# The last third of w_a and w_b in 512-column rows and one four-tile step, unit 4's output a slot earlier, and the last store on ACT's queue

One core of a Trainium2 chip. The metric is the device time of one execution in microseconds (us). The profiler's span of the core (first to last instruction) is 1.7 to 1.9 us shorter than that time. The kernel before takes 233.46 us (median of the five runs beside the changed kernel, 233.22 to 233.78).

## The reference

A blockwise decaying linear attention over q, k, v of shape (4, 8, 768, 64) is followed by a bilinear feed-forward network (FFN) over its 3072 x 512 output:

```python
# per head, in blocks of 64; o: (3072, 512) once transposed and flattened
out[:, :, sl] = intra + inter          # masked (q k^T) v, plus q times the running state
kv_state = lam_block * kv_state + kb_dec^T vb
...
a = x @ w_a                            # (3072, 512) @ (512, 1536)
b = x @ w_b
return (a * b @ w_out).astype(np.float32)
```

All inputs are float32. The kernel computes in bfloat16 and accumulates in float32.

## The kernel before

Tokens go in 24 units of 128, in groups of 4, 1, 2, 4, 4, 4, 4, 1 units. For each group the FFN makes twelve a tiles and twelve b tiles of 128 hidden columns (f = 0..11), the products ab, and then the output. The attention of later units is woven in at numbered slots. Only group 0 meets the weights while they arrive: 12 chunks of w_a and w_b (512 KB each, 256 columns over the whole contraction), then six of w_out. Each is loaded as float32 and cast to bfloat16. Engines go by the profiler's names: PE is TensorE (matmuls), DVE VectorE, ACT ScalarE, POOL GpSimd; SP (SyncE) issues nearly all transfers.

```python
W_CHUNKS = (256,) * 6
W_STEPS = ((0, 1), (2,), (3,), (4,), (5,))
PLAN = {0: [..., (26, "T", 4), (29, "C", 5), (29, "S", 4), (30, "PV", 4), (34, "O", 4), ...], ...}

for cs in W_STEPS:                                   # order of the loads
    pending += [("a", c) for c in cs] + [("b", c) for c in cs]
...
def load_w(kind, c):                                 # (cut: w_out)
    t = wst_pool.tile([128, 1024], F32, name="wst", tag="wst")
    t = t[:, :KS * w].rearrange("p (k n) -> p k n", k=KS)
    nc.sync.dma_start(out=t, in_=r[:, :, w_off[c]:w_off[c + 1]])
...
# ffn, group 0                                       # (cut)
for i, cs in enumerate(W_STEPS):
    nxt = W_STEPS[i + 1][0] if i + 1 < len(W_STEPS) else None
    a_sbs = [a_part(f, ...) for f in fs]             # matmuls; ACT evacuates a
    if i == 0: cast_w("b", cs[1], "act")
    elif nxt:  cast_w("a", nxt, "dve")
    for n_f, (f, a_sb) in enumerate(zip(fs, a_sbs)):
        b_part(f, xT, gt, a_sb, ab)                  # matmuls; DVE multiplies
        hook(f)
    if nxt: cast_w("b", nxt, "act")
for c in range(FC // 2):                             # output, slots 12 to 35
    for t in range(n):
        out_mms(ops[t], ab, t, range(2 * c, 2 * c + 2))
        if c == FC // 2 - 1: store(u0 + t, ops[t], 0, d_model)   # ACT copy, kept
        hook(slot); slot += 1
```

Before the loop over groups, POOL casts the first chunk of w_a ("a0") in two halves, and DVE casts a1 and b0. The "O" hook makes a unit's attention output on TensorE and copies it to the x tile (xT) on ACT.

## Time and profile before

| | before |
|---|---|
| time, us | 233.46 (233.22 to 233.78) |
| span, us | 231.5 |
| TensorE (PE) busy | 225.1 us, 97% |
| DVE / ACT / POOL busy | 50% / 39% / 22% |
| clock granted to PE | 0.998 |

A line of the timeline is: start, duration, engine, line of the kernel, operation, output<-inputs, shapes, count, and in brackets how long the engine had rested and on what. A matmul's end is a model: with 512 columns the matmuls start 0.216 us apart but each is shown 0.38 us long. I therefore read PE by its starts. The prediction shows the page's shares, the stretches and group 0. One piece that it does not show becomes important below, the start of group 0: the cast of a0 on POOL, the cast of b0 on DVE, and the first a and b matmuls.

```profile
16.82 0.61 POOL L162 CAST wa_sb<-wst 128x512 bf16<-128x512 f32 x1 [0.53 <-DMA wst<-in_moe_w_a_dram]
17.92 3.62 PE L439 MATMUL a_ps<-xT,wa_sb 128*128 128x384 bf16 x20 [0.23 <-ACT xT L362]
20.60 0.69 DVE L165 CAST wb_sb<-wst 128x1024 bf16<-128x1024 f32 x1 [1.61 <-DMA wst<-in_moe_w_b_dram]
21.39 1.03 PE L439 MATMUL b_ps<-xT,wb_sb 128*128 128x512 bf16 x4
```

POOL and DVE both rest until their chunk has landed. The first half of a0 is cast by 17.43, 0.49 us ahead of PE's start at 17.92. The cast of b0 ends at 21.29, only 0.10 us before PE uses it. In this execution neither is late, but b0 runs close.

### The profile page before, as it was taken

How to read it: one execution, taken by the hardware profiler on the slowest of the kernel's cores; microseconds unless marked ns; L12 is line 12 of the kernel's file. 1: busy time of each engine (PE TensorE's matmuls, PEld its weight loads, DVE VectorE, ACT ScalarE, POOL GpSimd, SP SyncE). 2: the span in 40 equal slices, each digit the busy share in tenths (PEclk: the TensorE clock that was granted, in tenths of full speed). 3: DMA queues.
4: the chain of work that ended last, by engine and by line, in shares of the span. 5: the costliest groups of instructions: out<-in, count | busy, mean ns of one | idle time of the engine just before them, and what ended most of it. 6: DMA issues, size and time to landing. Idle time of an engine off the chain costs nothing.

```text
span 231.5 us, 4532 instructions
## 1 busy us (share of the span) xinstructions
PE 225.1 (97%) x1779; PEld 124.8 (54%) x1779; DVE 115.9 (50%) x204; ACT 90.9 (39%) x172; POOL 50.8 (22%) x65
## 2 busy tenths in 40 slices
PE   7799999999999999999999999999999999999994
PEld 2484444459688654554544454544554544444493
DVE  0894757536469726676334584334483313331050
ACT  3677563066473243342233333233333234332261
POOL 6071000336564333334301533001200000000000
PEclk9999999999999999999999999999999999999999
DMA  4999999998999999999869995239300220000311
GB/s 154 303 281 349 349 364 301 299 189 189 204 229 161 225 195 217 213 184 213 304 201 203 218 175 113 93 103 194 66 3 0 91 93 0 1 0 23 115 45 50
DMA packets 96422, 38.84 MB, mean 168 GB/s; under 512 B 83344, under 2 KB 91920, under 8 KB 96400
## 3 DMA queue, kind: packets, MB, share of 16 engines
q1 hardware_dynamic: 96256, 38.54, 72.5%
q8 instruction: 14, 0.23, 0.4%
q14 instruction: 8, 0.07, 0.1%
q10 hardware_dynamic: 144, 0.00, 0.0%
HBM read 28.32 MB, written 6.29 MB: 149 GB/s over the span
## 4 chain that ended last, share of the span: by engine, by line
PE 87%; DMA 4%; SPq 3%; ACT 2%; DVE 1%; issue 0%
PE a_ps L439 27%; PE b_ps L439 26%; PE op L472 23%; PE o_ps L355 3%; DMA q<-in_q_dram 3%; PE kq L313 2%; SPq L129 2%; PE o_ps L345 2%; DMA qf<-in_q_dram 2%; PE kvd L369 2%; ACT scratch L565 1%; PE tps L299 1%; SPq L145 1%; DVE scratch L542 1%; PE kq L590 1%; ACT xT L362 0%
## 5 line engine op out<-in xcount | busy, mean ns | idle before, releaser
L452 DVE TENSOR_TENSOR ab<-a_sb,b_ps 128x512 bf16<-128x512 bf16 (+2 forms) x96 | 52.3, 552 | 78.4 <-PE b_ps L439 57.4
L439 PE MATMUL a_ps<-xT,wa_sb 128*128 128x512 bf16 (+3 forms) x388 | 77.0, 324 | 0.4 <-ACT xT L362 0.4
L439 PE MATMUL b_ps<-xT,wb_sb 128*128 128x512 bf16 (+2 forms) x384 | 77.1, 326 | 0.0
L447 ACT CAST a_sb<-a_ps 128x512 bf16<-128x512 f32 (+2 forms) x96 | 45.6, 481 | 62.6 <-PE a_ps L439 61.3
L472 PE MATMUL op<-wo_sb,ab 128*128 128x512 bf16 (+2 forms) x312 | 65.6, 363 | 0.0
L439 PEld LDWEIGHTS <-wb_sb 128*128 128x128 bf16 x384 | 34.5, 98 | 28.6 <-DVE wb_sb L165 0.3
L439 PEld LDWEIGHTS <-wa_sb 128*128 128x128 bf16 x388 | 34.0, 98 | 28.7 <-issue 0.8
L472 PEld LDWEIGHTS <-ab 128*128 128x128 bf16 x312 | 28.7, 98 | 29.9
L330 DVE TENSOR_TENSOR m<-kq,lotri 128x512 bf16<-128x512 f32 x47 | 29.3, 682 | 17.8 <-PE kq L313 17.2
L262 POOL TENSOR_TENSOR qk<-kf,lp_k 128x512 bf16<-128x512 f32 x18 | 19.3, 1074 | 74.8 <-DMA kf<-in_k_dram 58.2
L267 POOL TENSOR_TENSOR qk<-qf,lp_q 128x512 bf16<-128x512 f32 x20 | 21.9, 1095 | 23.3 <-DMA qf<-in_q_dram 23.3
L467 ACT COPY o_sb<-op 128x512 f32<-128x512 f32 (+2 forms) x19 | 10.3, 541 | 34.0 <-PE op L472 34.0
L362 ACT CAST xT<-o_ps 128x512 bf16<-128x512 f32 x22 | 12.0, 590 | 18.0 <-PE o_ps L355 17.5
L401 DVE TENSOR_TENSOR st<-kvd,bdiag 128x512 bf16<-128x512 f32 x18 | 12.3, 682 | 4.2 <-PE kvd L369 3.6
L276 DVE CAST vb<-vf 128x512 bf16<-128x512 f32 x17 | 9.7, 570 | 0.0
L301 ACT COPY qkT<-tps 128x1024 bf16<-128x1024 bf16 x5 | 5.1, 1012 | 9.9 <-PE tps L299 9.9
L198 PE MATMUL idle<-idle_sb 128*128 128x128 bf16 (+1 forms) x31 | 6.8, 359 | 1.3 <-DVE idle_sb L193 1.3
L355 PE MATMUL o_ps<-m,vb 128*64 128x128 bf16 x192 | 7.8, 222 | 0.0
L276 POOL CAST vb<-vf 128x512 bf16<-128x512 f32 x7 | 4.4, 631 | 13.1 <-DMA vf<-in_v_dram 13.1
L345 PEld LDWEIGHTS <-st 128*128 128x128 bf16 x80 | 5.4, 98 | 2.8
L313 PE MATMUL kq<-qkT 64*128 64x128 bf16 x160 | 6.6, 218 | 0.0
L355 PEld LDWEIGHTS <-vb 128*64 128x64 bf16 x192 | 5.7, 109 | 1.4
(57 smaller groups left out, 86.5 us busy)
## 6 DMA issues: line engine op xcount, KB each, us to landing
vf<-in_v_dram SPq DMA_DIRECT2D x24, 256.0 KB, 4.9
qf<-in_q_dram SPq DMA_DIRECT2D x20, 256.0 KB, 4.6
kf<-in_k_dram SPq DMA_DIRECT2D x20, 256.0 KB, 4.7
out_dram<-o_sb SPq DMA_DIRECT2D x16, 256.0 KB, 2.0
wst<-in_moe_w_a_dram SPq DMA_DIRECT2D x6, 512.0 KB, 8.6
wst<-in_moe_w_b_dram SPq DMA_DIRECT2D x6, 512.0 KB, 8.7
wst<-in_moe_w_out_dram SPq DMA_DIRECT2D x6, 512.0 KB, 8.6
out_dram<-o_kept SPq DMA_DIRECT2D x7, 256.0 KB, 2.5
```

The lines of the kernel that those rows point to most:

```text
L262: eng_of(eng).tensor_mul(qk[:, 1], raw.pop((u, "k")), lp_k[:, u % NB].to_broadcast([128, H, D]))
L267: eng_of(eng).tensor_mul(U[u]["qk"][:, 0], raw.pop((u, "q")), lp_q[:, u % NB].to_broadcast([128, H, D]))
L276: eng_of(eng).tensor_copy(vb, vf)
L313: nc.tensor.matmul(kq[i][:, hp, :], lhsT=d["kT"][p, hp, :], rhs=d["qT"][p, hp, :], start=True, stop=True, skip_group_check=True)
L330: nc.vector.tensor_mul(m, kq[i], lotri_bc)
L355: nc.tensor.matmul(d["o"][p, hp, :], lhsT=d["vb"][:, 2 * hp + i, :], rhs=d["m"](i, hp), start=(first and hp == 0), stop=True, skip_group_c ...
L362: nc.scalar.copy(xT[:, :, col:col + BLK], o_ps)
L401: nc.vector.tensor_mul(st[:].rearrange("p hp i d -> p hp (i d)"), ps[:].rearrange("p hp i d -> p hp (i d)"), bdiag_bc)
L439: nc.tensor.matmul(ps[:, lo:hi], lhsT=w_sb[:, s, f * 128:(f + 1) * 128], rhs=xT[:, s, lo:hi], start=(s == 0), stop=(s == KS - 1), skip_gro ...
L447: nc.scalar.copy(a_sb[:, :gt], ps[:, :gt])
L452: nc.vector.tensor_mul(ab[:, f, :gt], a_sb[:, :gt], ps[:, :gt])
L472: nc.tensor.matmul(op[:, lo:hi], lhsT=ab[:, f, t * 128:(t + 1) * 128], rhs=wo_sb[:, f, lo:hi], start=(f == 0), stop=(f == FC - 1))
```

## The change

Its intent: load the last third of w_a and w_b with longer contiguous rows, let ACT make unit 4's x tile before its two last closing copies of group 0, and spare the hop to SP's queue. Chunks 4 and 5 cover 512 columns (2 KB rows) over one half of the contraction each, so the last four f tiles become one step; "O" of unit 4 moves from slot 34 to 33; the last of the three closing stores is issued by ACT.

```diff
-W_STEPS = ((0, 1), (2,), (3,), (4,), (5,))
+W_STEPS = ((0, 1), (2,), (3,), (4, 5))
+W_HALVES = (4, 5)
@@ PLAN[0]
-        (26, "C", 4), (26, "T", 4), (29, "C", 5), (29, "S", 4), (30, "PV", 4), (34, "O", 4),
+        (26, "C", 4), (26, "T", 4), (29, "C", 5), (29, "S", 4), (30, "PV", 4), (33, "O", 4),
@@
+    def w_part(w, c):
+        if c in W_HALVES:
+            j = W_HALVES.index(c)
+            return w[:, 2 * j:2 * j + 2, w_off[W_HALVES[0]]:]
+        return w[:, :, w_off[c]:w_off[c + 1]]
@@ load_w
-            nc.sync.dma_start(out=t, in_=r[:, :, w_off[c]:w_off[c + 1]])
+            if c in W_HALVES:
+                t = t.rearrange("p k n -> p (k n)").rearrange("p (k n) -> p k n", k=2)
+            nc.sync.dma_start(out=t, in_=w_part(r, c))
@@ cast_w
-            dst = (wa_sb if kind == "a" else wb_sb)[:, :, w_off[c]:w_off[c + 1]]
+            dst = w_part(wa_sb if kind == "a" else wb_sb, c)
@@ store
-        nc.sync.dma_start(out=out_r[row][:, lo:hi], in_=o_sb[:, lo:hi])
+        (queue or nc.sync).dma_start(out=out_r[row][:, lo:hi], in_=o_sb[:, lo:hi])
@@ ffn, group 0 (cut)
-                nxt = W_STEPS[i + 1][0] if i + 1 < len(W_STEPS) else None
+                nxt = W_STEPS[i + 1] if i + 1 < len(W_STEPS) else ()
-                elif nxt:
-                    cast_w("a", nxt, "dve")
+                else:
+                    for c in nxt:
+                        cast_w("a", c, "dve")
-                if nxt:
-                    cast_w("b", nxt, "act")
+                for c in nxt:
+                    cast_w("b", c, "act")
@@ ffn, last group
-                    store(u0 + t, op, lo, hi)
+                    store(u0 + t, op, lo, hi, nc.scalar if hi == d_model else None)
```

More of the change, by code (lines that the diff above doesn't have):

```diff
@@ L458, in store_kept, with store @@
         nc.sync.dma_start(out=out_r[row], in_=o_sb)
-    def store(row, op, lo, hi):
+    def store(row, op, lo, hi, queue=None):
         if row < g_u0[KEEP_GROUPS]:
@@ L491, in ffn @@
                     if i == 0 and n_f == 1:
-                        cast_w("a", nxt, "dve")
-                if nxt:
-                    cast_w("b", nxt, "act")
+                        cast_w("a", nxt[0], "dve")
+                for c in nxt:
+                    cast_w("b", c, "act")
             ops = [ps_bank("op", [128, d_model], F32, hold=True) for _ in range(n)]
```

## The prediction

> **What bounds the kernel now.** I read the page first, its busy shares and its row of slices, to see which engine could be the bound and where it rests.
>
> ```profile
> PE 225.1 (97%) x1779; PEld 124.8 (54%) x1779; DVE 115.9 (50%) x204; ACT 90.9 (39%) x172; POOL 50.8 (22%) x65
> PE   7799999999999999999999999999999999999994
> PEclk9999999999999999999999999999999999999999
> DMA  4999999998999999999869995239300220000311
> ```
>
> TensorE works for 225.1 of 231.5 us at full clock. It is short of work only in the first two slices and the last. The DMA engines are saturated over the first fifth of the span, where the weights arrive, so the change works on a resource that is full. Whether it is on the path is another question, answered by the table of stretches, which I cut at the boundaries of the first FFN group (22.64 is the first b matmuls after its start, 50.40 its last output matmuls).
>
> ```profile
> 22.64:50.40 27.76, 27.76 (x150) 12.83 (x148) 17.84 (x27) 11.51 (x17) 3.77 (x4) 1.00 1.09 310
> 50.40:51.30 0.90, 0.73 (x10) 0.28 (x5) 0.00 (x0) 0.90 (x3) 0.00 (x0) 1.00 0.99 225
> 51.30:225.50 174.20, 174.20 (x1386) 97.49 (x1386) 84.51 (x154) 63.64 (x127) 38.63 (x37) 1.00 0.66 136
> 228.20:231.50 3.30, 0.00 (x0) 0.00 (x0) 0.00 (x0) 0.25 (x1) 0.00 (x0) 0.83 0.24 72
> ```
>
> The first numbers are length and PE busy: no hole from 22.64 to 50.40, all of the stage that waits for weights; one of 0.17 us at 51; none afterwards; and 3.3 us of tail without a matmul. Because matmul ends are modelled, I checked the pace of starts as well, in the timeline of PE:
>
> ```profile
> 28.62 1.89 PE L439 MATMUL a_ps<-xT,wa_sb 128*128 128x512 bf16 x8
> 30.35 1.89 PE L439 MATMUL b_ps<-xT,wb_sb 128*128 128x512 bf16 x8
> 32.08 1.89 PE L439 MATMUL a_ps<-xT,wa_sb 128*128 128x512 bf16 x8
> 33.80 1.89 PE L439 MATMUL b_ps<-xT,wb_sb 128*128 128x512 bf16 x8
> 35.53 1.89 PE L439 MATMUL a_ps<-xT,wa_sb 128*128 128x512 bf16 x8
> 37.26 1.89 PE L439 MATMUL b_ps<-xT,wb_sb 128*128 128x512 bf16 x8
> 50.46 0.61 PE L472 MATMUL op<-wo_sb,ab 128*128 128x512 bf16 x2
> 51.23 0.38 PE L439 MATMUL a_ps<-xT,wa_sb 128*128 128x128 bf16 x4 [0.17 <-ACT xT L362]
> ```
>
> Eight 512-column matmuls start every 1.725 us, so 0.216 us each, throughout the weights' arrival: no weight is ever late. The only wait near the change is the last line: the next group's first matmul waits for the x tile of unit 4.
>
> **What the Trainium skill says.** "TensorE: Matmul & The Clock Gate", section "Wait — 56ns, not 53.3ns?", gives a warm start-to-start of 215.7 ns at 512 columns; the trace's 0.216 us agrees, so the stage cannot run faster. "Trainium Kernel Development and Optimization", Key Constraints, says that DMAs from several engines' queues share the same 16 DMA engines and that this saves only issue time. No transfer of the kernel before shows it for a store (ACT's queue carried only a 4 KB load). "Perfetto Trace Analysis", the HWDGE part of the per-instruction lifecycle, says that a DMA's issue leaves out the data's movement and that the closing semaphore write can take surprisingly long for HBM; here the last store's issue took 0.33 us but its landing 1.7 us. No page that I read gives a gain for 2 KB rows over 1 KB ones, so that is taken from this trace.
>
> **Part 1: rows of 512 columns.** Four of the twelve a and b loads keep their 512 KB but go from 1 KB rows (256 columns of 4 bytes) to 2 KB rows. The trace holds both sorts, in the DMA view of 22 to 31 us (a and b) and of 32.5 to 37 us (almost only w_out, which has 2 KB rows):
>
> ```profile
> DMA packets 3143, 3.14 MB, mean 349 GB/s; under 512 B 95, under 2 KB 3142, under 8 KB 3142
> DMA packets 921, 1.73 MB, mean 386 GB/s; under 512 B 51, under 2 KB 97, under 8 KB 921
> ```
>
> 4 x 0.524 MB takes 6.01 us at 349 and 5.43 us at 386 GB/s. What follows lands about 0.6 us earlier. Nothing on PE waited for it, so on the path this is worth 0.
>
> **Part 2: one step of four f tiles instead of two steps of two.** Same matmuls, same casts of 128x1024 (0.69 us on DVE, 1.05 on ACT; the w_out casts already have the new two-by-512 form at 0.69). The order of loads becomes a4 a5 b4 b5. Each a pair is now two halves of the contraction, so the very first f tile of the step needs both. The deadlines, with landing as issue plus the DMA view's time to landing: a4 20.97 + 8.6 = 29.57, and the next three before at 31.0, 32.6 and 34.05. In the new order and at 1.36 us each: a5 about 30.8, b4 32.2, b5 33.6 (estimates). PE starts the step at 32.08 and needs the second half of wa two matmuls later, 32.5; DVE casts a5 from 30.8 to 31.5, so there is 1.0 us to spare. ACT now casts b4 and b5 before it evacuates the step's four a tiles: b5 from 33.6 to 34.65, against a need at 35.53 + 0.43 = 35.96, 1.3 us to spare. The four a evacuations, 0.52 us apart, then run from 34.65 to about 36.8. Their banks come round again seven allocations later, the first of them for the last b tile at about 38.1, so they are free. The a pool has five buffers for four tiles. DVE gets its four products bunched behind that: the first about 36.7 instead of 34.9, the last about 39.9, and the w_out casts between them stay ahead of use by about 1 us (third one done about 41.2, needed at 42.4). Every delay is inside slack, so this is worth 0 too.
>
> **Part 3: unit 4's output one slot earlier** (34 to 33). Now ACT's queue at the end of the group is:
>
> ```profile
> 49.13 1.56 ACT L463 COPY o_kept<-op 128x512 f32<-128x512 f32 x3 [2.01 <-PE op L472]
> 50.57 0.62 ACT L362 CAST xT<-o_ps 128x512 bf16<-128x512 f32 x1
> 51.15 0.59 ACT L463 COPY o_kept<-op 128x512 f32<-128x512 f32 x1
> ```
>
> Three kept copies stand before the x tile and only one pair of output matmuls (0.43 us) follows it on PE. After, two copies stand before and two pairs follow. The last output pair's stream ends at 50.46 + 0.43 = 50.89, while the next group starts at 51.23, so the true hole is **0.34 us** (the 0.17 in brackets counts from the modelled end). New: the o_ps matmuls end 0.43 earlier, about 50.03; ACT is done with the second copy about 50.17; x runs 50.17 to 50.79; PE is ready at 50.89. The hole closes. The masks it reads are done at 49.02 and the o_ps matmuls that read them would start about 49.7, so no new wait. ACT's last two copies move behind x and the next group's first a evacuation starts at about 51.7 as before, though PE is 0.34 ahead; its banks are then reused with 0.3 us or so to spare. Gain 0.34 us, at risk by about 0.1.
>
> **Part 4: the last store from ACT's queue.** ACT's last copy starts at 228.18, takes 0.27 and ends at 228.45; SP issues at 228.48. The hop is 0.03 us, and SP is not late: its issues at 227.24, 227.81 and 228.48 each take 0.33. Landing and closing handshake remain. Gain 0.0 to 0.05, and ACT's one earlier issue took 0.41 us, so it may as well lose 0.08. I take 0.
>
> **Sum.** 0 + 0 - 0.34 + 0: 233.46 - 0.34 = 233.1 us, or 0.15% less.
>
> **Rivals.** (a) The a halves come late: if 2 KB rows on these strided tensors ran no faster than 1 KB ones, a5 would land at 31.0 and be cast by 31.7, still 0.8 us early. Only a landing over 1 us later would make PE wait; then about 234. Against: the first eight loads and their issue times stay the same, and w_out shows the rate. (b) The bunched ACT and DVE work holds PSUM banks and the output matmuls wait: 0.3 to 1 us lost, 233.4 to 234.1. For it: ACT's four evacuations finish only when PE is at the second b tile, and group 1's bank reuse is tight. Against: all slacks above are positive. (c) The early weights let q, k and v arrive earlier and later stages speed up. Against: from 51.3 to 225.5 PE has no hole, so it is worth 0. (d) The queue that has been idle since the start is slower or faster to finish than SP's: 0.3 us either way, 232.8 to 233.4. Nothing in the trace speaks for it but that nothing rules it out.
>
> **Range and chances.** Runs before spread from 233.22 to 233.78, about 0.3 to either side. With rivals (b) and (d) on either side of 233.1, I give 232.5 to 233.7. A change of 2% is 4.7 us: faster would take more than the whole 3.3 us tail together with the hole, and slower would take a PE wait longer than any slack here. 0.01 each, 0.98 within 2%.
>
> **What would show it.** Right: DMA near 386 GB/s through 29 to 37 us, no PE wait on wa_sb or wb_sb in the four-tile step, the start of group 1 at about 50.9 with no wait on xT, everything after it 0.3 us earlier, and the tail from the last matmul to the end 3.3 us as now. Wrong: a wait of PE or its weight loads on a5's cast, an output matmul waiting on a_sb or ab, a new hole in the first microseconds of group 1, or a tail that differs by over 0.2 us. If the time differs from 233.1 by more than 0.6 us, one of these slacks was misjudged.

## The result

The changed kernel took 233.41 us (233.08 to 233.85, 5 runs) beside 233.46 of before. The ratio is 0.9997, 95% interval 0.9981 to 1.0013: no difference that these runs resolve. A ratio here is the mean time of one kernel's fast runs over that of the other's in the same rounds, so it is not quite the ratio of the quoted medians.

The four loads, as forecast, run faster. The DMA view of 29 to 36 us of the changed kernel:

```profile
DMA packets 1403, 2.71 MB, mean 387 GB/s; under 512 B 81, under 2 KB 81, under 8 KB 1403
```

The hole at 51 us has gone. ACT's queue and PE's timeline there, to be held against the lines of the prediction:

```profile
49.49 1.07 ACT L472 COPY o_kept<-op 128x512 f32<-128x512 f32 x2 [2.01 <-PE op L481]
50.50 0.58 ACT L371 CAST xT<-o_ps 128x512 bf16<-128x512 f32 x1
51.03 1.07 ACT L472 COPY o_kept<-op 128x512 f32<-128x512 f32 x2
...
50.39 1.04 PE L481 MATMUL op<-wo_sb,ab 128*128 128x512 bf16 x4
51.26 0.39 PE L448 MATMUL a_ps<-xT,wa_sb 128*128 128x128 bf16 x4
```

Four output matmuls start at 50.39 and stream until 50.39 + 4 x 0.216 = 51.25, and group 1 follows at 51.26. Yet group 1 starts at 51.26 and not at the 50.9 that was forecast, hardly different from 51.23 before. The 0.36 us had been lost ahead of it, at the start of group 0 (POOL's cast of a0 and PE's first a matmuls):

```profile
17.60 0.61 POOL L171 CAST wa_sb<-wst 128x512 bf16<-128x512 f32 x1 [1.13 <-DMA wst<-in_moe_w_a_dram]
18.27 3.64 PE L448 MATMUL a_ps<-xT,wa_sb 128*128 128x384 bf16 x20 [0.39 <-POOL wa_sb L171]
```

Here a0 landed 0.78 us later than in the trace of before, POOL's first half ended at 18.21, and PE began at 18.27 instead of 17.92. The question for the experiments is whether the change did that, or chance. Apart from this wait on POOL's cast, the view of PE's waits lists none from 17.9 to 52 us in the changed kernel.

### The profile page after: what moved, and what is told of

Its sections match the earlier page's. It is cut to its first block, busy times and chain, and to the rows that moved or that the text cites. A ratio compares the mean times of both kernels' runs of the same rounds, so it can differ in the third digit from the quotient of the medians.

```text
span 231.6 us, 4530 instructions
## 1 busy us (share of the span) xinstructions
PE 225.1 (97%) x1779; PEld 124.8 (54%) x1779; DVE 114.1 (49%) x204; ACT 90.6 (39%) x172; POOL 50.1 (22%) x65
## 4 chain that ended last, share of the span: by engine, by line
PE 91%; SPq 4%; DMA 3%; issue 0%; POOL 0%; ACT 0%
PE a_ps L448 27%; PE op L481 27%; PE b_ps L448 27%; SPq L130 3%; DMA wst<-in_moe_w_a_dram 3%; PE o_ps L364 3%; PE kq L322 2%; PE o_ps L354 2%; SPq L220 1%; PE kvd L378 1%; PE tps L308 1%; PE kvd L399 0%; POOL wa_sb L171 0%; ACT o_sb L476 0%
## 5 line engine op out<-in xcount | busy, mean ns | idle before, releaser
L448 PEld LDWEIGHTS <-wb_sb 128*128 128x128 bf16 x384 | 34.5, 98 | 28.6 <-ACT wb_sb L169 0.2
L276 POOL TENSOR_TENSOR qk<-qf,lp_q 128x512 bf16<-128x512 f32 x20 | 21.0, 1051 | 22.3 <-DMA qf<-in_q_dram 22.3
L371 ACT CAST xT<-o_ps 128x512 bf16<-128x512 f32 x22 | 12.0, 588 | 18.0 <-PE o_ps L364 17.5
L285 DVE CAST vb<-vf 128x512 bf16<-128x512 f32 x17 | 8.2, 482 | 0.0
```

What stands on the lines that cost most here:

```text
L276: eng_of(eng).tensor_mul(U[u]["qk"][:, 0], raw.pop((u, "q")), lp_q[:, u % NB].to_broadcast([128, H, D]))
L285: eng_of(eng).tensor_copy(vb, vf)
L371: nc.scalar.copy(xT[:, :, col:col + BLK], o_ps)
L448: nc.tensor.matmul(ps[:, lo:hi], lhsT=w_sb[:, s, f * 128:(f + 1) * 128], rhs=xT[:, s, lo:hi], start=(s == 0), stop=(s == KS - 1), skip_gro ...
```

## The experiments

The span is cut at four points that every PE timeline shows: the first b matmul of group 0, the first a matmul of group 1, the end of the last output matmul (its line's start plus its duration), and the end of the span (the trace has it to 0.01 us). "First b" stands for the start because it contains every wait for a0, a1 and b0. The four numbers of a row add up to the span.

| kernel | slot | loads | last store | first b | first b to group 1 | group 1 to last matmul | tail | span | median time |
|---|---|---|---|---|---|---|---|---|---|
| before | 34 | old | SP | 21.39 | 29.84 | 176.91 | 3.39 | 231.53 | 233.46 |
| changed | 33 | new | ACT | 21.75 | 29.51 | 176.90 | 3.48 | 231.64 | 233.41 |
| slot_only | 33 | old | SP | 21.59 | 29.53 | 177.03 | 3.38 | 231.53 | 233.33 |
| loads_only | 34 | new | SP | 21.59 | 29.85 | 177.04 | 3.36 | 231.84 | 233.46 |
| store_only | 34 | old | ACT | 23.75 | 29.85 | 176.90 | 3.48 | 233.98 | 233.81 |
| store_again | 34 | old | ACT | 21.60 | 29.86 | 176.91 | 3.46 | 231.83 | 233.54 |
| after_again | 33 | new | ACT | 21.61 | 29.52 | 176.91 | 3.45 | 231.49 | 233.20 |
| slot_loads | 33 | new | SP | 21.97 | 29.51 | 176.91 | 3.36 | 231.75 | 233.28 |
| rows_1kb | 33 | four-tile step, 1 KB rows | ACT | 21.73 | 29.51 | 177.00 | 3.48 | 231.72 | 233.40 |
| late_half | 33 | new, a5 one load later | ACT | 21.51 | 30.03 | 176.91 | 3.45 | 231.90 | 233.56 |
| later_half | 33 | new, a5 two loads later | ACT | 21.54 | 31.14 | 177.34 | 3.46 | 233.48 | 235.33 |
| split_first | 33 | new, a0 and b0 in halves | SP | 22.39 | 29.52 | 176.91 | 3.38 | 232.20 | 233.60 |

Each row's first five numbers are from one execution, its median from that kernel's four to six. The first four experiments ran together on one chip, where before was 233.53 us (11 runs, 233.40 to 233.64).

**slot_only**: before, with `(33, "O", 4)`.

> The kernel before with unit 4's output at slot 33 and nothing else. Main theory: this is the only part of the change on the path. From the first a matmul of group 0 to the end of the last output matmul the trace shows 210.2 us before and 209.9 after; here 209.9, with no wait on xT at about 51 us, so the mean time is 0.3 us under before, as far as the start of group 0 (17.9 or 18.3 us, set by when the first w_a chunk lands) does not hide it. Rival (the loads or the four-tile step are what closed the hole): 210.2 with the 0.2 us wait on xT still there.

Measured: 233.33 us, ratio 0.9992 (0.9980 to 1.0004). The total by itself does not resolve the gain, since the interval includes 1. The stretch to group 1 does: it is 29.53 against 29.84 of before, and group 1 now starts right after the four output matmuls (50.24 + 4 x 0.216 = 51.10), so the slot alone closes the hole:

```profile
50.24 1.04 PE L472 MATMUL op<-wo_sb,ab 128*128 128x512 bf16 x4
51.12 0.39 PE L439 MATMUL a_ps<-xT,wa_sb 128*128 128x128 bf16 x4
```

The whole run from first a matmul to last output was 210.21, though, and not 209.9: this execution gave the gain back at b0. The cast of b0 on DVE and the first b matmuls of slot_only:

```profile
20.84 0.69 DVE L165 CAST wb_sb<-wst 128x1024 bf16<-128x1024 f32 x1 [1.50 <-DMA wst<-in_moe_w_b_dram]
21.59 1.04 PE L439 MATMUL b_ps<-xT,wb_sb 128*128 128x512 bf16 x4
```

The first a matmul was at 17.94, so PE was free at about 21.41 (the 3.47 us of before's first part); b0 landed 0.24 us later than in the trace of before, its cast ended at 21.53 and PE waited until 21.59. A further 0.12 us went after group 1, a spread that loads_only shares.

**loads_only**: the changed kernel with slot 34 and the last store on SP.

> The kernel before with the 512-column loads and the four-tile step, unit 4's output at slot 34, last store by SP. Main theory: the DMA rate rises to about 385 GB/s from 29 us on, but from the first a matmul to the last output matmul it is 210.2 us as before, with the xT wait still at 51 us; time equal to before within 0.1 us. Rival (bunched casts or the later products cost something that the slot gave back): over 210.4 us.

Measured: 233.46 us, ratio 0.9998 (0.9985 to 1.0011), 387 GB/s over 29 to 36 us, 29.85 us to group 1, and the wait on xT still there:

```profile
50.66 0.61 PE L481 MATMUL op<-wo_sb,ab 128*128 128x512 bf16 x2
51.44 0.38 PE L448 MATMUL a_ps<-xT,wa_sb 128*128 128x128 bf16 x4 [0.17 <-ACT xT L371]
```

In group 0 the loads and the four-tile step cost nothing and bring nothing. From the first a matmul to the last output matmul it is 210.36 us, between the 210.2 of the main theory and the 210.4 of the rival. The excess lies after group 1: the third number, 177.04, is on the upper side of a spread (176.90 to 177.04) that I did not explain. It is not put down to the loads, since slot_only has it without them and after_again and slot_loads do not have it with them.

**after_again**: the changed kernel unaltered.

> The changed kernel once more. Main theory: first a matmul to last output matmul 209.9 us again; the start of group 0 may be anywhere from 17.9 to 18.4 us since the instructions ahead of it are those of before and only the landing of the first w_a chunk moves it; time 0.0 to 0.35 us under before. Rival (the change itself makes that chunk land late): the start is at 18.3 in this run too, while slot_only and store_only start at 17.9.

Measured: 233.20 us (233.17 to 233.27), ratio 0.9988 (0.9976 to 0.9999). The first a matmul started at 17.91, so the late a0 of the first trace was not the change's doing; b0 was the late one here (cast from 20.86, first b at 21.61), and from the first a matmul to the last output matmul it is 210.13 us instead of the 209.9 expected. The same program thus gave a first b of 21.75 and of 21.61. Over the ten traces whose first loads came punctually (all but store_only and split_first), first b moves from 21.39 to 21.97 with the same instructions ahead of it, so this is chance in the landing of the first chunks. Before's trace, with 21.39, is the earliest of all.

**store_only and store_again**: before, with only the last store on ACT.

```diff
-                    store(u0 + t, op, lo, hi)
+                    store(u0 + t, op, lo, hi, nc.scalar if hi == d_model else None)
```

> The kernel before with the last store issued by ACT. Main theory: first a matmul to last output matmul stays 210.2 us; the tail from the last matmul's end to the end of the span stays 3.3 to 3.4 us (3.36 before, 3.44 after), time equal to before within 0.1 us. Rival (the hop to SP matters, or ACT's queue is slow to finish): tail shorter or longer by over 0.2 us.

Measured: 233.81 us (233.59 to 235.69), ratio 1.0027 (1.0004 to 1.0050), so the time was not within 0.1 us of before. The profiled execution was the one of 235.69 us; there the very first load of q landed late, and so everything did (PE's waits of store_only):

```profile
PE tq L554 <- DVE scratch L542: 2.5, 2, 2.2
```

Its tail, 3.48 (3.3 to 3.4 was expected), says more than its time. The other executions of this batch were slow too, and they left no trace.

> The kernel before with the last store issued by ACT, once more, since its first run started late and its five timed runs were 0.3 us over before. Main theory: the tail from the last matmul's end to the span's end is 3.45 to 3.5 us against 3.36 to 3.39 with SP (three profiles), so the time is 0.1 us over before; the rest of the first result was chance in the start. Rival (ACT's queue costs more than the profile shows): 0.25 us or more over before again.

Measured: 233.54 us beside 233.57, ratio 1.0001 (0.9989 to 1.0014). The excess did not come back. Why the first batch was slow stays open beyond its one trace. The tail does repeat: 3.36 to 3.39 us in the five profiles with SP, 3.45 to 3.48 in the seven with ACT, so ACT's store costs 0.09 us. The last copy and store, before and changed:

```profile
228.18 0.27 ACT L467 COPY o_sb<-op 128x128 f32<-128x128 f32 x1 [0.40 <-PE op L472]
228.48 0.33 SPq L468 DMA_DIRECT2D out_dram<-o_sb  x1
```

```profile
228.21 0.27 ACT L476 COPY o_sb<-op 128x128 f32<-128x128 f32 x1 [0.41 <-PE op L481]
228.50 0.36 ACTq L477 DMA_DIRECT2D out_dram<-o_sb  x1
```

From the copy's start to the issue it is 0.30 us with SP and 0.29 with ACT: there was no hop to save. The issue is 0.03 us longer, but that is already part of the time to the landing. From the start of the issue to the landing, the packed traces have 1.60 to 1.66 us in the five with SP and 1.65 to 1.68 in the seven with ACT (the views round both to 1.6 or 1.7), 0.03 us more on average. The other 0.05 us or so falls between the landing and the end of the span (1.41 us on average with SP, 1.46 with ACT). Why is not shown.

**rows_1kb**: the four-tile step with 256-column chunks over the whole contraction.

```diff
-W_HALVES = (4, 5)
+W_HALVES = ()
```

> The changed kernel with the same four-tile step and order of loads, but rows of 256 columns (1 KB) for all chunks, each over the whole contraction. Main theory: the DMA runs on at 349 GB/s until 32 us instead of rising to about 385 at 29, the w_out chunks land about 0.5 us later, and the time is that of the changed kernel within 0.1 us: row length is off the path. Rival (the faster rows are worth something): slower by 0.3 us or more.

Measured: 233.40 us beside 233.57; ratio of the means 1.0002 (0.9987 to 1.0018), since one of its four runs took 234.09. First b to group 1 is 29.51, as with 2 KB rows. The DMA moved 368 GB/s over 29 to 36 us (1 KB rows first, then w_out) against 387. Over 29 to 32.5 us, where nearly all rows are 1 KB in rows_1kb and 2 KB in the changed kernel, with the same step and order, the views show (rows_1kb, then changed):

```profile
DMA packets 1184, 1.23 MB, mean 350 GB/s; under 512 B 45, under 2 KB 1126, under 8 KB 1184
DMA packets 697, 1.36 MB, mean 387 GB/s; under 512 B 35, under 2 KB 35, under 8 KB 697
```

With the step and the order of loads kept, the rate follows the row length. DVE could start the last w_out cast at 44.80 instead of 43.88 in the changed kernel, 0.9 us later where 0.5 was expected. PE's stretch shows neither: row length is off the path.

**late_half and later_half**: the last four loads in another order.

```diff
-    for cs in W_STEPS:
+    for cs in W_STEPS[:-1]:
         pending += [("a", c) for c in cs] + [("b", c) for c in cs]
+    pending += [("a", 4), ("b", 4), ("a", 5), ("b", 5)]   # later_half: a4 b4 b5 a5
```

> The changed kernel with the last four weight loads in the order a4 b4 a5 b5, so that the second half of the contraction for w_a lands one load (1.36 us) later. In the profile after, its cast ended at 31.6 us and the third matmul of the four-tile step was due at 32.9, 1.3 us to spare. Main theory (slack, not the path): here the cast ends at about 32.95 and the wait of TensorE on it is at most 0.2 us; time within 0.2 us of the changed kernel's. Rival (no such slack, the DMA sets the pace of this stage): time up by 1 us or more.

> The changed kernel with the order a4 b4 b5 a5, so that the second half of w_a lands two loads (2.7 us) later. Main theory: the slack of 1.3 us is used up and TensorE waits about 1.4 us at the third matmul of the four-tile step, and all of it reaches the end: time up by 1.3 to 1.5 us over the changed kernel's. Rival (a later slack takes it up, or the order of landing does not matter): under 0.5 us.

Measured: late_half 233.56 us (ratio to before 1.0002, 0.9988 to 1.0015), stretch 30.03, 0.52 longer than the 29.51 of the kernels with the slot: over the 0.2 us that I allowed. In that execution a5's cast started at 32.39, 1.49 us later than in the changed kernel (not 1.36), and PE had started the step 0.23 us earlier than there, so the 1.28 us to spare (cast ended 31.59, due 32.44 + 0.43) became -0.44. later_half 235.33 us (1.0080, 1.0067 to 1.0094), stretch 31.14, 1.63 longer, and 0.43 more later on. The four-tile step and the later wait in later_half:

```profile
32.23 0.59 PE L449 MATMUL a_ps<-xT,wa_sb 128*128 128x512 bf16 x2
34.27 3.19 PE L449 MATMUL a_ps<-xT,wa_sb 128*128 128x512 bf16 x14 [1.45 <-DVE wa_sb L174]
```

```profile
PE a_ps L449 <- DVE wa_sb L174: 1.5, 1, 1.5
...
PE o_ps L355 <- DVE st L411: 0.3, 1, 0.3
```

Exactly two matmuls run on the first half of the contraction, then PE waits for the second. So the slack was real and about as large as worked out; once it is used up, the wait lengthens the stretch by as much (in late_half PE goes on at 33.14, 0.50 us after it was due, and the stretch is 0.52 longer), and in later_half a later wait of another unit's attention on DVE adds to it. I had expected 1.3 to 1.5 us and saw about 2.

**slot_loads**: the changed kernel with the last store on SP.

> The changed kernel with the last store back on SP. Theory from the traces so far: the stretch from the first b matmul to the first a matmul of group 1 is 29.5 us (29.5 with slot 33, 29.85 with slot 34 in every trace), the tail 3.36 to 3.39 us (with ACT's store 3.45 to 3.48), so the time is 0.1 us under the changed kernel's and 0.35 to 0.45 under before, give or take 0.2 us of chance in when the first weights land. Rival (the tail differs for another reason): tail 3.45 or more again.

Measured: 233.28 us beside 233.56 of before, ratio 0.9986 (0.9973 to 1.0000). Stretch 29.51 and tail 3.36, as expected. The time is 0.28 us under before, under the 0.35 to 0.45 expected but inside the 0.2 us of chance allowed; the profiled execution had the latest start of the punctual ones (first b 21.97, since a1's cast ended only at 20.17). By the parts it should beat the changed kernel by 0.09 us; the runs do not resolve that.

**split_first**: slot_loads, with a0 and b0 each loaded as two halves of 128 columns and b0 cast in two.

> Slot 33, the 512-column loads and SP's last store, and the first chunk of w_a and of w_b each loaded as two halves of 128 columns, b's cast in two as well. Theory: in nearly all traces the start of group 0 waits for the landing or cast of one of the first weight chunks, so that the first b matmul starts at 21.5 to 21.75 instead of 21.4. With the first halves landing about 0.7 us earlier it starts at 21.4 (first a matmul at 17.9), and the time is 0.1 to 0.3 us under slot_loads. Rival (512-byte rows are so much slower that the second halves and the next chunk come later): first b matmul at 21.7 or later, time no better.

Measured: 233.60 us beside 233.56, ratio 1.0008 (0.9995 to 1.0021). It did not help. This execution was also 0.7 us late from the first load of q on, so its first b of 22.39 is not comparable as it stands; but from its own first a matmul (18.72) to first b it took 3.67 us instead of 3.47. The casts of a1 and of b0's first half:

```profile
19.91 0.69 DVE L180 CAST wa_sb<-wst 128x1024 bf16<-128x1024 f32 x1 [0.90 <-DMA wst<-in_moe_w_a_dram]
20.81 0.43 DVE L180 CAST wb_sb<-wst 128x512 bf16<-128x512 f32 x1 [0.21 <-DMA wst<-in_moe_w_b_dram]
```

a0 and b0's halves were in time, but a1, behind the two halves of a0, was not: its cast ended at 20.60, due at 18.72 + 1.73 = 20.45. Over 14.5 to 17.5 us the DMA moved 282 GB/s here and 331 to 350 in the traces with whole first chunks and a punctual start. That window favours the punctual ones: store_only, with whole chunks and a start 2.4 us late, has 287. In the window 0.7 us later (15.2 to 18.2), which makes up for the late start, it is 308 here and 350 to 357 in the punctual traces, so most of the loss of rate stays. The rival of the expectation was thus right as far as this one trace goes: with shorter rows the wait moved to the next chunk.

## Why the prediction was right

The time, 233.41, lies within 232.5 to 233.7. That alone says little: the range holds the time before (233.46) too, and in the first comparison chance at the start hid nearly all of the forecast gain. The forecast difference of 0.34 us is 0.15%, less than a single batch resolves; the stretches settle the steps.

- *Part 1 (rows), worth 0*: right. The rate was 387 GB/s where 386 was taken from w_out, and rows_1kb and loads_only show that nothing on PE waits for it.
- *Part 2 (four-tile step), worth 0*: right, with its landing times. Casts of a5, b4 and b5 started at 30.90, 32.25 and 33.59 where 30.8, 32.2 and 33.6 were estimated. late_half and later_half show that the slack exists and where it ends: 1.28 us in the changed kernel where 1.0 was worked out.
- *Part 3 (slot), worth 0.34*: right. The stretch is 0.31 to 0.35 us shorter in the traces that have slot 33 and are otherwise undisturbed, and slot_only shows that the slot alone does it. The feared wait on reused banks in group 1 did not come: group 1 to the last matmul stays within 176.90 to 177.04.
- *Part 4 (last store), taken as 0*: mis-sized. It costs 0.09 us. The prediction named the size ("may as well lose 0.08") and then chose 0. The agreement of 0.08 with 0.09 is luck: the 0.08 was the longer issue of a load, and the issue of this store is only 0.03 longer.
- *"No weight is ever late"*: true of the one trace that it was read from, where b0 was cast 0.10 us ahead of its use, but wrong for the first three chunks in most other executions. The check of PE's pace began at 28.6 us. In nine of the eleven traces besides before's, a0, a1 or b0 decided when PE's first b matmul began, and landings that moved by some tenths from execution to execution hid the gain in the first comparison. Of the rivals, none named this; (a) asked only about the last third.

The sum of the parts as measured in the traces is -0.33 + 0.09 = -0.24 us for the changed kernel, with some 0.2 us of chance either way: after_again lies 0.33 us under before, the first batch 0.05. slot_loads, without the ACT store, should gain 0.33 and lies 0.28 under. Of these three totals only after_again's interval (0.9976 to 0.9999) stays clear of 1.

## What to carry to other kernels

A transfer that keeps all DMA engines busy may still be off the path: look at the starts on the bounding engine before paying for a faster transfer, and find the slack by landing a load late on purpose. A gain of a few tenths of a microsecond cannot be seen in the total when the first loads land with that much spread; cut the span at fixed instructions and compare the stretches. Test parts singly even when the whole is neutral: here one part gave 0.33 us, one cost 0.09, and one did nothing.

## What the Trainium skill lacked or had wrong

- "DMA: Bandwidth & Descriptors", Specifications, puts line rate at transfers of at least 512 B and the HBM limit of a core at about 358 GB/s. Here 1 KB rows, well above 512 B, ran at 349 to 350 GB/s and 2 KB rows at 387 on the same queue, in a program on one core, both with the DMA engines full (busy share 1.09 and 1.05 in the table of stretches). "Perfetto Trace Analysis", Roofline, does say that a single core can exceed 358. The pages do speak of an overhead of small DMAs and small packets, so longer rows should help; a measured rate by row length for this chip I found in none.
- "Trainium Kernel Development and Optimization", Key Constraints, says that issuing from several engines saves only the sequencer's issue time. For one closing store there was nothing to save, and ACT's queue cost 0.09 us in the tail (3.45 to 3.48 us in seven profiles against 3.36 to 3.39 in five). No page that I read has this.
- "Perfetto Trace Analysis", the Tensor Engine part of the per-instruction lifecycle, says that a matmul's end is estimated. It does not say what that hides: a hole of 0.34 us was listed as 0.17, and a wait of about 0.2 us for b0's cast was not listed for PE at all.
- No page that I read speaks of the spread of landings at launch: the first b matmul, behind the same instructions, started between 21.39 and 21.97 us in ten traces, and in one trace, where the first load of q came late, at 23.75.
